# Two engines make the low words' integers, and GpSimd scales both heads' value products

## The chip, the cores and the metric

The kernel runs on one core of one Trainium2 chip. The metric is the device time of one execution in microseconds (us). The engines are named as in the profile: PE is TensorE (matmuls; PEld its weight loads), DVE is VectorE, ACT is ScalarE, POOL is GpSimd, and SP is the engine that only issues DMAs here. Each engine works through its own queue in order; between engines, semaphores hold an instruction back until what it needs is done.

## The reference

```python
# attention: 8 batches, 8 heads, 576 tokens, head size 64, all float32
scores = scale * np.matmul(q, k.transpose(0, 1, 3, 2))
thresh = np.max(scores, axis=-1, keepdims=True) - tau
scores = np.where(scores >= thresh, scores, -1000000000.0)
scores = scores - np.max(scores, axis=-1, keepdims=True)
attn = np.exp(scores)
attn = attn / (np.sum(attn, axis=-1, keepdims=True) + 1e-09)
attn_out = np.matmul(attn, v)
# heads joined: x is 4608 x 512; w_in 512 x 2048 and w_out 2048 x 512 come as float64
h = np.maximum(x @ w_in, 0.0)
return (h * h @ w_out).astype(np.float32)
```

## The kernel before

The kernel has two halves. The first is attention, the second a feed-forward layer on nine blocks of 512 tokens, whose matrix products are cut into sums and products of blocks (lines 813 to 867 for the hidden layer, 931 to 993 for the output).

Attention is a software pipeline written out by hand. A pair of heads and a block of 128 queries make a unit; two units, A and B, make one period, and `period(p)` runs for p from -2 to 74. A period issues its steps in the order of a list of names: `CONVERTING` in the periods in which a chunk of the weights is converted (p = 2 to 34), `PLAIN` in the others. This order is the order of each engine's queue; nothing reorders it later. The steps that matter here are:

- `SA`, `SB`: score products of the units A and B on PE (line 434). `topA0` to `topB1`: DVE takes each head's extreme value from PSUM and copies the scores to SBUF (line 452). `leastA`, `leastB`: POOL adds tau (line 459). `powA0` to `powB1`: the exponentials on ACT (line 462). `maskA0` to `maskB1`: DVE multiplies by the threshold's mask and sums the row (line 467).
- `over`, `inv`: POOL adds 1e-9 to the sums of the period before, and DVE takes the reciprocal (lines 474, 477).
- `U`, `V`, `W`: PE turns the weights of earlier units into PSUM (line 380), `eU`, `eV`, `eW`: ACT copies them to SBUF (line 523). `T`, `eT`: the same for queries and keys (lines 398, 403, 411); `eT` also asks for later loads.
- `PV`: the value products on PE, into PSUM banks 0 and 5 (line 532), the banks from which `topA0` and `topA1` read. `x`: they are scaled by the reciprocals, which lie in `wT` behind the turned weights (lines 640 to 646). `xm`: POOL's part of the scaling, and the stores of the result (lines 649 to 658).
- `fetch`, `c1` to `c6`: conversion of the weights from float64 to float32, one chunk of 128x512 in a period, 32 chunks in all (m = 0 to 31, begun in period m + 2). The chunk lies in SBUF as pairs of 32-bit words, low and high. `c1` takes the absolute value of the high words (ACT, line 205), `c3` clamps it (POOL, line 219), `c4` shifts it left by three (DVE, line 227), `c5` joins it with sign and top bit (DVE, line 235). `c2` makes an integer out of the top three bits of the low word, by a multiplication with 2^-29 (ACT, line 212). `c6` adds the two as integers (POOL, line 245), into the weights' place or into a tile that SP then stores.

In a converting period one of the two value products is copied by ACT and multiplied by POOL, and the other is multiplied by DVE straight from PSUM. `raw` (the two words) has four buffers, `a` (the high word) three, `x` two.

Of the kernel before, what the change touches and what calls it, by code (L numbers as in the profile page):

```python
# [11 lines left out]
I32 = mybir.dt.int32  # L12
U32 = mybir.dt.uint32
ALU = mybir.AluOpType
AF = mybir.ActivationFunctionType
# [33 lines left out]
def kernel(  # L49
# [25 lines left out]
    nc = tc.nc  # L75
    B, H, S, D = q.shape
    P = 128
# [25 lines left out]
    sb, cv = Region(arena, 0, X_AT[0]), Region(arena, X_AT[0], ARENA)  # L103
# [49 lines left out]
    WC = 512  # L153
# [16 lines left out]
    blocks_out = [(m, k) for k in RAW for m in RAW]  # L170
    chunks += [(W_OUT, m, k, out_blocks[m, k]) for m, k in blocks_out[:EARLY]]
    is_wide = moe_w_in.dtype != FP32
    raws, parts = {}, {}

    def weight(m):
        return weight_tile(*chunks[m][0:3])
# [32 lines left out]
    def convert2(m):  # L209
        if m in parts:  # L210
            lo = parts[m][0]
            nc.scalar.activation(out=lo, in_=lo.bitcast(U32), func=AF.Copy, bias=0.0, scale=2.0**-29)

    def convert3(m):
        if m not in parts:
            return
        a = parts[m][2].bitcast(FP32)
        low, high = (0x38000000, 0x47EFFFFF)
        nc.gpsimd.tensor_scalar(  # L219
            out=a, in0=a, scalar1=as_float(high), scalar2=as_float(low), op0=ALU.min, op1=ALU.max  # L220
        )

    def convert4(m):
        if m not in parts:
            return
        lo, hi, a = parts[m]
        nc.vector.tensor_scalar(
            out=a, in0=a, scalar1=3, scalar2=0x3FFFFFFF, op0=ALU.logical_shift_left, op1=ALU.bitwise_and
        )
# [255 lines left out]
    wT = {}  # L485

    TURNS = {}
    for g in range(2, 2 * len(pairs)):
        two, x = divmod(g - 4, 4)
# [4 lines left out]
    SCALE_AT = 10  # L494
# [4 lines left out]
    def fill(m, f, pt, at=None):  # L499

        first, count = FILLS[f]
        if m not in wT:
            wT[m] = sb.tile([P, (2 * CH + 2) * P], FP32, tag="wT", bufs=W_RING, name="wT")
        for i, (u, c) in enumerate(FIRST[first : first + count]):
            half_turn(pt, i, weights[2 * m + u][:, c, :, :].rearrange("p j d -> p (j d)"), at)
        if f == "W":
            rs = smalls.pop(m)
            for j in range(2):
                for r in range(2):
                    rows = ds(r * HALF, HALF)  # L510
                    for u in range(2):
                        one = rs[rows, 3, 2 * u + j : 2 * u + j + 1]
                        wide = bass.AP(tensor=one.tensor, offset=one.offset, ap=[one.ap[0], [0, D]])
                        to = pt[ds(u * D, D), r, ts(count + j, HALF)]
                        made = nc.tensor.matmul(to, wide, ident[rows, rows], start=True, stop=True)  # L515
                        touch("turns", made, at and at + r * BANK, BANK)

    def filled(m, f, pt, at=None):

        first, count = FILLS[f]  # L520
        count += 2 * (f == "W")
        to = wT[m][:, ds(weight_at(first) * P, count * P)]
        touch("weights", nc.scalar.copy(joined(to), whole(pt, 0, count)), at, 2 * BANK, m)  # L523
# [15 lines left out]
    def valued(m):  # L539

        for u in range(2):
            n = 2 * m + u
            weights.pop(n)
            if units[n][1] == FULL:
                for i in units[n][0]:
                    loaded_v.pop(i)
                    if i + 3 < len(pairs):
                        load_v(i + 3)
# [10 lines left out]
    def has(n):  # L559
        return 0 <= n < NU  # L560
# [5 lines left out]
    def sums_due(p):  # L566

        return p > max(starts) and not converts(p)
# [14 lines left out]
    def converts(p):  # L583
        return is_wide and (has_chunk(p) or has_chunk(p - 1))

    def has_chunk(p):
        return p in starts

    def begun(n):
        return starts.get(n)  # L590
# [4 lines left out]
        maskB1  # L595
    """.split()
    CONVERTING = """
        fetch U SA s1 eU over topA1 topA0 leastA SB c1 topB0 V c2 PV topB1 powA1 powA0
        eV powB1 maskA1 T leastB inv c3 powB0 W maskA0 x c4 maskB1 c5 maskB0 c6 xm eT eW
    """.split()  # L600

    def spots():
        return [(sc[:, ds(b * BANK + REST, (FULL + 1) * HALF)], b * BANK) for b in (1, 4)]

    def middle():
        return sc[:, 2 * BANK : 4 * BANK].rearrange("p (r n) -> p r n", r=2)

    def period(p):

        A, B_, a, b = 2 * p, 2 * p + 1, 2 * p - 2, 2 * p - 1  # L610
        m, turns = p - 2, TURNS.get(p, ())
        late, pt = {"W": []}, {}

        def fills(f, m):
            if has(2 * m):
                pt[f] = pt_pool.tile([P, 2, BANK], FP32, tag="pt", name="pt")
                fill(m, f, pt[f])

        def evict(f, m):
            if has(2 * m):  # L620
                filled(m, f, pt[f], 2 * BANK if f == "W" else None)

        def W():
            if has(2 * m + 2):
                pt["W"] = middle()
                fill(m + 1, "W", pt["W"], 2 * BANK)

        def turn_some():
            late["turn"] = [turn(g // 2, g % 2, spots()) for g in turns]

        def PV():
            if has(2 * m):
                values(m)

        def values_out():
            if not has(2 * m):
                return
            late["x"] = x = sb.tile([P, 2, P], FP32, tag="x", bufs=2, name="x")
            for j in range(2):
                from_ = sc[:, ds(5 * j * BANK, P)]  # L640
                if converts(p) and j == 0:
                    made = nc.scalar.copy(x[:, j, :], from_)
                else:
                    made = nc.vector.tensor_tensor(  # L644
                        out=x[:, j, :], in0=from_, in1=wT[m][:, ts(SCALE_AT + j, P)], op=ALU.mult
                    )
                touch("x", made, 5 * j * BANK, P, m)

        def given_out():
            if has(2 * m):  # L650
                x = late.pop("x")
                if converts(p):
                    mine = x[:, 0, :]
                    nc.gpsimd.tensor_tensor(out=mine, in0=mine, in1=wT[m][:, ts(SCALE_AT, P)], op=ALU.mult)
                wT.pop(m)
                valued(m)
                give_x(m, x)
            ask(False)

        def scored_a():  # L660
            if has(A):
                scores(A, False)
                scores(A, True)
                scores(B_, True)
                softmax(A)

        def scored_b():
            if has(A):
                scores(B_, False)
                softmax(B_)  # L670

        def every(key):
            for then in late.get(key, ()):
                then()

        steps = {
            "U": lambda: fills("U", m), "V": lambda: fills("V", m + 1), "W": W, "T": turn_some,
            "eU": lambda: evict("U", m), "eV": lambda: evict("V", m + 1), "eW": lambda: evict("W", m + 1),
            "eT": lambda: every("turn"),
            "SA": scored_a, "SB": scored_b,  # L680
            "PV": PV, "x": values_out, "xm": given_out,
            "c1": lambda: convert1(begun(p)), "c2": lambda: convert2(begun(p)),
            "c3": lambda: convert3(begun(p - 1)), "c4": lambda: convert4(begun(p - 1)),
            "c5": lambda: convert5(begun(p - 1)), "c6": lambda: convert6(begun(p - 1)),
            "s1": lambda: sums_due(p) and sums_step(), "s2": lambda: sums_due(p) and p < 60 and sums_step(), "fetch": lambda: fetch(begun(p + 2)),
        }
        steps["over"] = lambda: do(a, "over")
        steps["inv"] = lambda: do(a, "inverse")
        for letter, n in (("A", A), ("B", B_)):
            for what, name in (("least", "least"),):  # L690
                steps[what + letter] = lambda n=n, name=name: do(n, name)
            for what, name in (("top", "top"), ("pow", "power"), ("mask", "mask")):
                for j in range(2):
                    steps[f"{what}{letter}{j}"] = lambda n=n, name=name, j=j: do(n, name, j)
        for name in CONVERTING if converts(p) else PLAIN:
            steps[name]()
        for n in (A, B_):
            if has(n) and units[n][1] == FULL:
                for i in units[n][0]:
                    turned.pop(i)  # L700
# [489 lines left out]
def as_float(bits):  # L1190
    import struct

    return struct.unpack("<f", struct.pack("<I", bits))[0]
# [30 lines left out]
```

## Time and profile before

| what | value |
|---|---|
| median of 2 runs | 1316.74 us (1316.07 to 1317.4) |
| profiled execution, its own time | 1314.57 us |
| span of its profile | 1312.8 us, 47885 instructions |
| busy over the span: PE / DVE / ACT / POOL | 1271.9 / 1007.1 / 855.8 / 872.0 us |
| TensorE clock granted | 0.999 of full speed |
| line 212 (c2) | 32 times, first at 24.6 us, last at 252.0 us |

The profile is of one execution. A group of instructions is shown by line, engine, operation, and what it writes and reads; then the count, the busy time in us and the mean in ns of one, and the idle time of the engine ahead of them with what ended it. Almost all SBUF tiles are parts of one tensor, `arena`, and `wall` holds the weights. A row of the timeline gives start and duration in us.

### The profile page before, as it was taken

To read this page: it belongs to the slowest core of one execution; us is meant where nothing else is said; L and a number is where in the kernel's file an instruction comes from. 1 tells how busy PE (TensorE), PEld (TensorE's weight loads), DVE (VectorE), ACT (ScalarE), POOL (GpSimd) and SP (SyncE) were. 2 spreads that over 40 slices of the span, in tenths; PEclk is the share of its full clock that TensorE was granted. 3 is DMA by queue.
4 is the path that set the end of the run, shared out by engine and by line. 5 is a ranking of instruction groups with operands and counts; after the bars stand their busy time and mean duration, and the time that the engine had idled before them with its cause. 6 is when DMAs were issued, how large, how long until landed. Compare 5 with 4: busy or idle time off the path is not lost.

```text
span 1312.8 us, 47885 instructions
## 1 busy us (share of the span) xinstructions
PE 1271.9 (97%) x19483; PEld 1142.1 (87%) x19483; DVE 1007.1 (77%) x2464; ACT 855.8 (65%) x1497; POOL 872.0 (66%) x991
## 2 busy tenths in 40 slices
PE   8998989899999999999999999999999999999998
PEld 5666666677777777999999999999999999999998
DVE  5999999999999996877887788777656654665463
ACT  6999999988999986566756675665524322432240
POOL 1556555565555421778887888758777777777775
PEclk9999999999999999999999999999999999999999
DMA  5465566544433312466556655669745224522411
GB/s 150 105 176 153 153 177 179 153 113 103 99 78 84 79 42 47 148 209 198 183 184 209 200 188 176 194 229 387 260 161 161 63 99 162 161 65 97 161 33 33
DMA packets 247035, 192.12 MB, mean 146 GB/s; under 512 B 97184, under 2 KB 195488, under 8 KB 246816
## 3 DMA queue, kind: packets, MB, share of 16 engines
q1 hardware_dynamic: 245504, 188.66, 47.6%
q8 instruction: 153, 2.51, 0.8%
q14 instruction: 66, 0.54, 0.1%
q10 hardware_dynamic: 1312, 0.41, 0.1%
HBM read 116.65 MB, written 72.35 MB: 144 GB/s over the span
## 4 chain that ended last, share of the span: by engine, by line
PE 74%; DVE 7%; issue 6%; ACT 3%; POOL 3%; DMA 3%; SPq 0%; POOLq 0%; DVEq 0%; ACTq 0%
PE ph L825 30%; PE po L960 29%; PE sc L532 6%; PE sc L434 5%; DVE arena L452 4%; PE pt L380 3%; POOL arena L219 2%; DVE arena L467 2%; ACT arena L462 1%; ACT arena L523 1%; DVE arena L235 1%; PE sc L398 1%; DMA xT<-arena 1%; PE sc L515 1%; DMA wall<-w 1%
## 5 line engine op out<-in xcount | busy, mean ns | idle before, releaser
L125 POOL TENSOR_TENSOR arena<-arena 128x512 f32<-128x512 f32 (+1 forms) x314 | 378.1, 1223 | 133.6 <-DVE arena L125 115.8
L960 PE MATMUL po<-wall,arena 128*128 128x128 f32 x3528 | 394.8, 275 | 1.4 <-ACT arena L737 1.4
L960 PEld LDWEIGHTS po<-wall,arena 128*128 128x128 f32 x3528 | 394.3, 192 | 1.9 <-ACT arena L737 1.8
L825 PE MATMUL ph<-arena,wall 128*128 128x128 f32 x3528 | 394.2, 275 | 0.7 <-DVE arena L644 0.7
L825 PEld LDWEIGHTS ph<-arena,wall 128*128 128x128 f32 x3528 | 394.0, 192 | 0.8 <-issue 0.8
L125 DVE TENSOR_TENSOR arena<-ph,arena 128x512 f32<-128x512 f32 x378 | 256.4, 689 | 86.2 <-PE ph L825 65.4
L122 POOL TENSOR_TENSOR arena<-arena 128x128 f32<-128x128 f32 (+2 forms) x314 | 254.8, 812 | 49.1 <-DMA arena<-w 32.9
L125 DVE TENSOR_TENSOR arena<-po,arena 128x128 f32<-128x128 f32 x378 | 108.4, 290 | 167.8 <-PE po L960 163.4
L467 DVE SCALAR_TENSOR_TENSOR arena<-arena 128x576 f32<-128x576 f32 x288 | 229.5, 818 | 0.7 <-POOL arena L459 0.5
L462 ACT ACTIVATE arena<-arena 128x576 f32<-128x576 f32 x288 | 207.9, 772 | 15.6 <-DVE arena L452 11.4
L452 DVE TENSOR_SCALAR_CACHE_REDUCE arena<-sc 128x576 f32<-128x576 f32 x288 | 205.4, 751 | 15.8 <-ACT arena L523 4.6
L771 ACT COPY c<-arena 128x512 f32<-128x512 f32 (+1 forms) x303 | 174.0, 581 | 50.2 <-DVE arena L122 41.5
L532 PEld LDWEIGHTS sc<-arena 64*64 64x64 f32 x5760 | 153.7, 133 | 50.1 <-DVE arena L452 37.2
L532 PE MATMUL sc<-arena 64*64 64x128 f32 (+1 forms) x5760 | 169.8, 262 | 19.4 <-DVE arena L452 18.8
L122 DVE TENSOR_TENSOR arena<-arena,c 128x512 f32<-128x512 f32 (+1 forms) x267 | 175.1, 664 | 6.2 <-ACT c L771 4.1
L434 PE MATMUL sc<-arena 64*64 64x64 f32 (+1 forms) x2304 | 167.1, 414 | 6.7 <-ACT arena L403 4.0
L523 ACT COPY arena<-pt 128x1024 f32<-128x1024 f32 x144 | 146.1, 1015 | 27.0 <-PE pt L380 26.7
L737 ACT COPY arena<-po 128x128 f32<-128x128 f32 x63 | 16.7, 265 | 186.2 <-PE po L960 183.4
L459 POOL TENSOR_SCALAR arena<-arena,tau_p 128x2 f32<-128x2 f32 x144 | 74.8, 520 | 81.1 <-DVE arena L452 77.9
L380 PEld LDWEIGHTS pt<-ident,arena 64*128 64x128 f32 x2304 | 83.4, 138 | 43.9 <-ACT arena L523 27.5
L737 ACT COPY arena<-ph 128x512 f32<-128x512 f32 x63 | 36.7, 582 | 123.5 <-PE ph L825 122.9
L380 PE MATMUL pt<-ident,arena 64*128 64x64 f32 x2304 | 102.6, 228 | 5.9 <-ACT arena L523 4.7
(50 smaller groups left out, 892.0 us busy)
## 6 DMA issues: line engine op xcount, KB each, us to landing
g<-arena SPq DMA_DIRECT2D x144, 256.0 KB, 2.6
arena<-g SPq DMA_DIRECT2D x144, 256.0 KB, 4.4
w<-arena SPq DMA_DIRECT2D x60, 256.0 KB, 2.4
wall<-w SPq DMA_DIRECT2D x49, 256.0 KB, 5.2
arena<-w SPq DMA_DIRECT2D x44, 256.0 KB, 3.3
arena<-in_v_dram SPq DMA_DIRECT2D x32, 288.0 KB, 3.8
out_dram<-arena SPq DMA_DIRECT2D x70, 128.0 KB, 2.2
arena<-in_q_dram SPq DMA_DIRECT2D x64, 128.0 KB, 3.5
```

What stands on the lines that cost most here:

```text
L122: e.tensor_tensor(out=out, in0=x, in1=y, op=ALU.subtract)
L125: e.tensor_tensor(out=out, in0=x, in1=y, op=ALU.add)
L380: made = nc.tensor.transpose(pt[:, r, ts(slot, HALF)], of[rows, :], ident[rows, rows])
L434: made = nc.tensor.matmul(sc[at, ds(to, count)], lhs, kT[rows, ds(at_k, count)], start=True, stop=True)
L452: made = nc.vector.tensor_scalar(out=s[:, j, :], in0=sc[:, ds(at, S)], scalar1=1.0, scalar2=None, op0=ALU.mult, op1=ALU.min, accum_out=nmx ...
L462: nc.scalar.activation(out=w[:, :, j, :], in_=of(j), func=AF.Exp, bias=nmx[:, j : j + 1], scale=-1.0)
L467: nc.vector.scalar_tensor_tensor(out=w[:, :, j, :], in0=of(j), scalar=thr[:, j : j + 1], in1=w[:, :, j, :], op0=ALU.is_le, op1=ALU.mult, a ...
L523: touch("weights", nc.scalar.copy(joined(to), whole(pt, 0, count)), at, 2 * BANK, m)
L532: made = nc.tensor.matmul(sc[ds(u * D, D), ds(5 * j * BANK + row, count)], loaded_v[i][rows, (c - (u != j)) % CH, :], wT[m][rows, ds(weigh ...
L771: nc.scalar.copy(c, y)
L825: nc.tensor.matmul(to[:, j, :], W_IN[m, k][:, ts(j, P)], of[k][:, m - 1, :], start=(not more and j == 0), stop=True, skip_group_check=True,)
L960: nc.tensor.matmul(to, g[:, j, :], w[:, j, :], start=(not more and j == 0), stop=(j == 3), skip_group_check=True)
```

## The change

`c2` of each chunk becomes five instructions. ACT writes its integer to a tile `t` (one buffer) instead of in place. POOL makes the same integer from the same low word by a multiplication, in place over the low word. POOL subtracts ACT's integer from its own, DVE shifts the difference left by 24, and POOL adds the shifted difference to the low word's integer, which `c6` adds to the high word one period later.

In converting periods both value products are copied by ACT, and POOL multiplies both at once (128x256 instead of 128x128); DVE's multiplication is left out there. `c3` works on the chunk begun in the same period instead of the one before. The list `CONVERTING` has another order, among other things with `c2` behind `c5` and `eV` and ahead of `maskB1`, with `T` ahead of `SB`, `over` behind `leastA`, and `inv` behind `c4`. `PLAIN` and the second half are as they were; `convert_out` has no chunks left to convert, since all 16 of `w_out` are among the 32.

```diff
--- before.py
+++ after.py
@@ -170,7 +170,7 @@
     blocks_out = [(m, k) for k in RAW for m in RAW]
     chunks += [(W_OUT, m, k, out_blocks[m, k]) for m, k in blocks_out[:EARLY]]
     is_wide = moe_w_in.dtype != FP32
-    raws, parts = {}, {}
+    raws, parts, differs = {}, {}, {}
 
     def weight(m):
         return weight_tile(*chunks[m][0:3])
@@ -209,7 +209,15 @@
     def convert2(m):
         if m in parts:
             lo = parts[m][0]
-            nc.scalar.activation(out=lo, in_=lo.bitcast(U32), func=AF.Copy, bias=0.0, scale=2.0**-29)
+            t = cv.tile([P, WC], I32, tag="t", bufs=1, name="t")
+            differs[m] = t
+            nc.scalar.activation(out=t, in_=lo.bitcast(U32), func=AF.Copy, bias=0.0, scale=2.0**-29)
+            nc.gpsimd.tensor_scalar(out=lo, in0=lo.bitcast(U32), scalar1=2.0**-29, scalar2=None, op0=ALU.mult)
+            nc.gpsimd.tensor_tensor(out=t, in0=lo, in1=t, op=ALU.subtract)
+            nc.vector.tensor_scalar(
+                out=t, in0=t, scalar1=24, scalar2=-1, op0=ALU.logical_shift_left, op1=ALU.bitwise_and
+            )
+            nc.gpsimd.tensor_tensor(out=lo, in0=lo, in1=t, op=ALU.add)
 
     def convert3(m):
         if m not in parts:
@@ -595,8 +603,8 @@
         maskB1
     """.split()
     CONVERTING = """
-        fetch U SA s1 eU over topA1 topA0 leastA SB c1 topB0 V c2 PV topB1 powA1 powA0
-        eV powB1 maskA1 T leastB inv c3 powB0 W maskA0 x c4 maskB1 c5 maskB0 c6 xm eT eW
+        fetch SA U eU T SB topA0 s1 c1 topA1 topB0 c3 V PV leastA over powA0 topB1
+        powA1 powB0 c4 eT inv x maskA1 maskA0 W leastB maskB0 c5 eV c2 powB1 c6 eW maskB1 xm
     """.split()
 
     def spots():
@@ -638,7 +646,7 @@
             late["x"] = x = sb.tile([P, 2, P], FP32, tag="x", bufs=2, name="x")
             for j in range(2):
                 from_ = sc[:, ds(5 * j * BANK, P)]
-                if converts(p) and j == 0:
+                if converts(p):
                     made = nc.scalar.copy(x[:, j, :], from_)
                 else:
                     made = nc.vector.tensor_tensor(
@@ -650,8 +658,8 @@
             if has(2 * m):
                 x = late.pop("x")
                 if converts(p):
-                    mine = x[:, 0, :]
-                    nc.gpsimd.tensor_tensor(out=mine, in0=mine, in1=wT[m][:, ts(SCALE_AT, P)], op=ALU.mult)
+                    both = x[:, :, :].rearrange("p j n -> p (j n)")
+                    nc.gpsimd.tensor_tensor(out=both, in0=both, in1=wT[m][:, ds(SCALE_AT * P, 2 * P)], op=ALU.mult)
                 wT.pop(m)
                 valued(m)
                 give_x(m, x)
@@ -680,7 +688,7 @@
             "SA": scored_a, "SB": scored_b,
             "PV": PV, "x": values_out, "xm": given_out,
             "c1": lambda: convert1(begun(p)), "c2": lambda: convert2(begun(p)),
-            "c3": lambda: convert3(begun(p - 1)), "c4": lambda: convert4(begun(p - 1)),
+            "c3": lambda: convert3(begun(p)), "c4": lambda: convert4(begun(p - 1)),
             "c5": lambda: convert5(begun(p - 1)), "c6": lambda: convert6(begun(p - 1)),
             "s1": lambda: sums_due(p) and sums_step(), "s2": lambda: sums_due(p) and p < 60 and sums_step(), "fetch": lambda: fetch(begun(p + 2)),
         }
```

## The prediction

> **What bounds the kernel now.** I read the busy table of the page first, then the windows of the two halves of attention, because the change only touches periods in which weight chunks are converted.
>
> ```profile
> PE 1271.9 (97%) x19483; PEld 1142.1 (87%) x19483; DVE 1007.1 (77%) x2464; ACT 855.8 (65%) x1497; POOL 872.0 (66%) x991
> ```
> ```profile
> 45.00:265.00 220.00, 197.84 (x5171) 140.81 (x5168) 209.26 (x602) 212.33 (x367) 129.06 (x180) 1.00 0.58 161
> 270.00:500.00 230.00, 226.29 (x5977) 170.28 (x5973) 221.69 (x661) 205.33 (x319) 113.47 (x162) 1.00 0.36 83
> ```
>
> The columns of the second fence are window, length, and busy time of PE, PEld, DVE, ACT, POOL. Over the whole span PE looks like the bound; from 45 to 265 us, where chunks are converted, it is not: ACT is busy 212.3 of 220 us and DVE 209.3, PE only 197.8. POOL is busy 129.1, so 90.9 us idle.
>
> ```profile
> L212 ACT ACTIVATE arena<-arena x32: 652/722/755, 24.6 to 252.0; 128x512 int32<-128x512 uint32 x32
> ```
>
> The step that is changed (c2, line 212) runs 32 times, first at 24.6 and last at 252.0 us. One converting period is therefore (252.0 - 24.6)/31 = 7.34 us. Per period (30 of them in 220 us) ACT works 7.08 us, DVE 6.98, POOL 4.30; POOL is idle 3.03 us. So there is some 0.3 us of slack on ACT and DVE, and 3 us on POOL.
>
> ```profile
> L219 POOL TENSOR_SCALAR arena<-arena 128x512 f32<-128x512 f32 x30 | 34.3, 1145 | 0.0
> L459 POOL TENSOR_SCALAR arena<-arena,tau_p 128x2 f32<-128x2 f32 x60 | 30.0, 499 | 31.5 <-DVE arena L452 28.8
> L245 POOL TENSOR_TENSOR arena<-arena 128x512 int32<-128x512 int32 x15 | 23.1, 1540 | 28.4 <-DVE arena L235 26.5 <-DMA arena<-in_k_dram 1.9
> L654 POOL TENSOR_TENSOR arena<-arena 128x128 f32<-128x128 f32 x30 | 13.6, 452 | 0.0
> ```
>
> These groups of POOL in that window are the price list. Last I read one period in the timeline, for the spacing of the instructions on one engine and the hand-offs between engines.
>
> ```profile
> 182.32 0.25 ACT L642 COPY arena<-sc 128x128 f32<-128x128 f32 x1
> 182.65 0.43 DVE L227 TENSOR_SCALAR arena<-arena 128x512 int32<-128x512 int32 x1 [0.30 <-POOL arena L219]
> 182.95 1.02 ACT L523 COPY arena<-pt 128x1024 f32<-128x1024 f32 x1
> 183.00 0.81 DVE L467 SCALAR_TENSOR_TENSOR arena<-arena 128x576 f32<-128x576 f32 x1
> ...
> 184.34 0.81 DVE L467 SCALAR_TENSOR_TENSOR arena<-arena 128x576 f32<-128x576 f32 x1
> 184.45 0.70 ACT L212 ACTIVATE arena<-arena 128x512 int32<-128x512 uint32 x1
> 184.51 1.53 POOL L245 TENSOR_TENSOR arena<-arena 128x512 int32<-128x512 int32 x1 [1.89 <-DVE arena L235]
> ...
> 185.08 0.75 DVE L452 TENSOR_SCALAR_CACHE_REDUCE arena<-sc 128x576 f32<-128x576 f32 x1
> ...
> 185.75 0.75 DVE L452 TENSOR_SCALAR_CACHE_REDUCE arena<-sc 128x576 f32<-128x576 f32 x1
> ...
> 186.57 2.36 PE L532 MATMUL sc<-arena 64*64 64x64 f32 x108 [0.71 <-DVE arena L452]
> ...
> 186.88 0.29 POOL L459 TENSOR_SCALAR arena<-arena,tau_p 128x2 f32<-128x2 f32 x1
> ...
> 188.04 0.72 POOL L459 TENSOR_SCALAR arena<-arena,tau_p 128x2 f32<-128x2 f32 x1 [0.87 <-DVE arena L452]
> ```
>
> What to see: DVE starts 0.03 us after the POOL result it waits for (181.47 + 1.15 to 182.65); a line 227 holds DVE 0.35 us until the next start, a mask (467) 0.74, a maximum (452) 0.67; the value products (532) start 0.82 us after the start of the second maximum and take 2.36 us. No step of today's c2 waits for POOL: the integer is one ACT instruction and is next read a period later.
>
> **The change, part by part.**
>
> *Value products.* The second 128x128 scaling leaves DVE (line 644, 8.6 us over 30, so 0.29 us) and becomes an ACT copy (line 642, 0.25 us). POOL's multiplication grows from 128x128 (0.45 us) to 128x256. Its price lies between 0.45 and twice that; between 0.45 at 128 elements and 1.28 at 512 (line 122 in the timeline at 308 us) a straight line gives 0.73, which I take. ACT would come to 7.33 us per period, just its present length.
>
> *Difference step.* Per chunk three POOL instructions of 128x512 and one DVE instruction come in. DVE's shift has the form of line 227: 0.43 us, 0.35 between starts. POOL's subtraction and addition are integer two-input operations like line 245: upper end 1.54. That row starts 0.17 us after a mask starts on DVE, and behind a mask POOL is slower (line 459: 0.29 us beside a maximum, 0.72 beside a mask, 0.43 more), so the lower end is 1.54 - 0.43 = 1.11; line 122's 1.28 lies between. I take 1.4. POOL's multiplication (uint32 to int32) appears in no row; line 219, one input, takes 1.15 beside a mask and so 0.72 without; the conversion could add up to line 245's 1.54. I take 1.0, nearer to line 219.
>
> POOL's work per period: 4.30 + (0.73 - 0.45) + 1.0 + 2 x 1.4 = 8.4 us, where 7.34 were available. At the upper prices it is 9.2. That alone ends the cover of 3.03 us.
>
> The Trainium skill (GPSIMD Engine Reference, section 3.1) puts a two-input GpSimd operation at some 2.6 cycles per element; as an estimate at its 1.2 GHz that is 1.11 us for 512 elements, the lower end above, and the loop below would be 0.3 us shorter with it.
>
> *The waits are dearer than the work*, as c2 now stands before the last mask. POOL's multiplication writes in place over the low words that ACT's c2 reads, so it waits for ACT's c2. The DVE shift waits for POOL's subtraction, and behind the shift on DVE stand maskB1 and all maxima of the next period. POOL's addition waits for the shift. From the end of one subtraction to the next:
> - hand-off 0.03, shift 0.35, maskB1 0.74, topA0 0.67, and 0.82 from topA1's start to the value products: 2.61 us. The products write the banks that these two maxima read, so they can't start sooner.
> - value products 2.36: 4.97.
> - hand-off 0.05 (taken), two ACT copies x, 0.15 between starts (182.32 to the next ACT start at 182.47): 5.32.
> - eV, which stands ahead of c2 on ACT: 0.95 of its 1.02; then c2 0.72: 6.99. All other ACT work (powers, eT, eU, c1) fits into the 4.97 us before x.
> - hand-off to POOL 0.08 (line 235's end to line 245's start), multiplication 1.0, 0.1 to the dependent one, subtraction 1.4: 9.57 us.
>
> POOL's own queue in the meantime: addition, c6, the scaled products, c3, leastA, over, leastB, from 0.5 us after the subtraction: 1.4 + 1.5 + 0.73 + 1.15 + 0.29 + 0.23 + 0.72 = 6.0, so it reaches the multiplication at 6.5, before ACT releases it at 7.1. DVE gets `over` at about 5.8 and does inv, three masks and c5 (0.09 + 3 x 0.74 + 0.61) by 8.7, before the shift is due at 9.6. So the mixed loop sets the period.
>
> *Other moves.* c3 moves into the chunk's own period, off DVE's path: line 227 loses its 0.30 us wait (9.2 us over 31). That is inside the new loop's slack, hence nothing. T, eT and the loads issued in them come earlier, `over` and leastA later: DVE idles until `over` anyway. SP's queue: the stores behind c6 and xm wait longer, but x and the raw chunk have two and four buffers, and all loads are two periods ahead; without that cover it would cost a transfer's 2 to 4 us once.
>
> **The sum.** 9.57 - 7.34 = 2.23 us per period, times 32 chunks = 71 us. 1314.6 us (the profiled execution, span 1312.8) + 71 = 1386; the median of the two runs lies 2.2 us above the profiled one, so 1388. With lower prices (0.72 and 1.11) the loop is 9.0 us: +53, 1370. With upper ones (1.54 and 1.54) 10.25: +93, 1410. The periods after line 252 us and the second half (PE at 100%) are untouched.
>
> **The rivals.**
> 1. *POOL and DVE shut each other out.* Line 459's 0.29 against 0.72 is such a case. With POOL nearly always at work, four masks, c4 and c5 would each hold a POOL instruction up: POOL's chain at full rows is 1.15 + 0.29 + 0.23 + 0.72 + 1.15 + 1.54 + 0.5 + 1.54 + 1.54 + 0.73 = 9.4 us with three such delays in it; three more of 0.43 make 10.7. +3.35 x 32 = 107: 1424 us. Against it: in the loop above the masks fall where POOL does small work or waits. The Trainium skill (SBUF — State Buffer, "Who interferes with whom") states this as a rule: a DVE instruction with two SBUF inputs and a GpSimd one that reads SBUF block each other for a whole instruction. Line 459 agrees; whether a long POOL instruction holds a mask back as fully isn't in these rows.
> 2. *POOL's added work is short.* If multiplication and subtraction took 0.45 and 0.7 us (a 128x128's price plus a little), the loop is 7.07 + 1.25 = 8.3 us: +31, 1348. For it: a part of line 245's 1.54 is waiting. Against it: line 122 takes 1.28 with no mask beside it.
> 3. *Not slower.* The integers are wanted only a period later (c6), so the chain might hide in POOL's 3.03 idle us, with DVE and ACT still setting 7.34. Place: the shift's wait on DVE. This decides if c2's end to the shift's start costs under 7.34 - 7.07 = 0.27 us. For it: POOL at 59%. Against it: the order in DVE's queue puts the next maxima behind that wait. It would give about 1317, or 1308 if also the 0.3 us waits for line 219 go.
> That the difference is all zeros would not change the time: every instruction still runs.
>
> **How the numbers follow.** Forecast 0.72 (its own range 1362 to 1412), rival 1 0.17, rival 2 0.07, rival 3 0.04. The predicted time is the forecast's, 1388 us. The range 1350 to 1425 takes in rival 1 and most of rival 2. A measurement tells about 2% here, 1290 to 1343 us: faster 0.02, same 0.05, slower 0.93.
>
> **What would show it.** Right: the new shift starts 9.3 to 10.2 us after its predecessor; DVE's largest wait in 45 to 300 us is this shift on POOL's subtraction; POOL's multiplication waits for ACT's c2; ACT and DVE fall to some 75% busy there; the windows of the last 900 us keep their shape. The step on the loop is wrong if POOL shows no idle time ahead of the multiplication (POOL's own chain then bounds), and the sizes are wrong if the subtraction isn't 1.1 to 1.55 us. A period under 8 us would refute the forecast.

## The result, and the profile after

The changed kernel takes 1433.93 us (median of 2 runs, 1432.61 to 1435.26) against 1316.74 us: ratio 1.0889, 95% interval 1.0863 to 1.0915. The profiled execution has a span of 1430.7 us, 117.9 more than before. It is slower, as forecast, but 46 us beyond the predicted 1388 and 9 us outside the range.

First two lines of the page: busy time of PE over the whole span, and the clock that TensorE was granted in 40 equal slices.

```profile
PE 1331.0 (93%) x19483; PEld 1192.4 (83%) x19483; DVE 1019.5 (71%) x2463; ACT 862.7 (60%) x1530; POOL 1011.9 (71%) x1087
...
PEclk9988899878899999999999999999999999999999
```

Before, every digit of the clock was 9. Now PE is 59 us longer busy with the same 19483 matmuls, and sevens and eights of the clock stand among the first eleven slices, which hold the converting periods.

The windows of attention after the change (window, length, busy time of PE, PEld, DVE, ACT, POOL, then the granted clock):

```profile
45.00:265.00 220.00, 165.49 (x3503) 121.48 (x3506) 152.82 (x412) 150.17 (x269) 178.19 (x185) 0.90 0.40 102
...
420.00:620.00 200.00, 197.37 (x5236) 148.80 (x5227) 192.29 (x580) 178.51 (x277) 94.78 (x137) 1.00 0.34 79
```

In the converting stretch ACT and DVE fell from 212.3 and 209.3 of 220 us to 150.2 and 152.8: neither is the bound any more. POOL is busy 178.2 us, yet idle for 42. Once no chunk is left (420 to 620 us) PE is busy 99% of the time at clock 1.00, as it was before in such periods (226.3 of 230 us).

The new shift (line 217) with what its engine waited for, from the view of one line (minimum, median, maximum in ns; first and last start):

```profile
L217 DVE TENSOR_SCALAR arena<-arena x32: 426/427/429, 34.7 to 375.0; 128x512 int32<-128x512 int32 x32
its engine sat idle before it (us, times) until:
  POOL arena L216: 83.4, 32
```

The shift waits 2.6 us per chunk for POOL's subtraction. POOL's multiplication (line 215) takes 1.60 to 2.08 us, 1.65 in the median, and waits 1.5 us per chunk for ACT's c2. A period is (375.0 - 34.7)/31 = 10.98 us on average, where 9.57 was forecast. In stretches at full clock it is 9.95. One such period in the timeline:

```profile
193.60 0.43 ACT L650 COPY arena<-sc 128x128 f32<-128x128 f32 x2
193.92 1.03 ACT L531 COPY arena<-pt 128x1024 f32<-128x1024 f32 x1
194.82 0.71 ACT L214 ACTIVATE arena<-arena 128x512 int32<-128x512 uint32 x1
195.61 1.60 POOL L215 TENSOR_SCALAR arena<-arena 128x512 int32<-128x512 uint32 x1 [0.55 <-ACT arena L214]
...
195.66 1.23 DVE L475 SCALAR_TENSOR_TENSOR arena<-arena 128x576 f32<-128x576 f32 x1
...
197.30 1.36 POOL L216 TENSOR_TENSOR arena<-arena 128x512 int32<-128x512 int32 x1
...
198.69 0.43 DVE L217 TENSOR_SCALAR arena<-arena 128x512 int32<-128x512 int32 x1 [1.17 <-POOL arena L216]
199.03 0.81 DVE L475 SCALAR_TENSOR_TENSOR arena<-arena 128x576 f32<-128x576 f32 x1
199.20 1.81 POOL L220 TENSOR_TENSOR arena<-arena 128x512 int32<-128x512 int32 x1 [0.54 <-DVE arena L217]
...
199.91 0.20 PEld L388 LDWEIGHTS pt<-ident,arena 64*128 64x128 f32 x4 [1.97 <-DVE arena L475]
```

This is the loop of the prediction, in its order: copies x (650), eV (531), c2 (214), multiplication, subtraction, shift, maskB1. The last line is new to the argument: PE, which has to turn the weights that maskB1 makes, waits 2 us for it.

The other periods differ from this one almost only in the value products (line 540). The same 70 of them in a period at half clock and in this one, and the windows around the two, where the third column from the end is the granted clock:

```profile
90.38 3.77 PE L540 MATMUL sc<-arena 64*64 64x128 f32 x70 [0.25 <-DVE arena L460]
191.32 2.19 PE L540 MATMUL sc<-arena 64*64 64x128 f32 x70 [0.25 <-DVE arena L460]
```
```profile
90.30:93.70 3.40, 3.32 (x64) 3.32 (x67) 2.33 (x9) 2.24 (x5) 3.24 (x6) 0.50 0.10 19
191.00:194.00 3.00, 2.53 (x75) 2.15 (x74) 2.04 (x7) 2.88 (x8) 2.94 (x6) 1.00 0.08 17
```

From topA1's start to the end of the value products it is 3.01 us in the periods at full clock, 3.94 on average over 31 periods, and up to 4.9. These 0.93 us are most of the 1.03 between 9.95 and 10.98. That the 2 us waits bring the low clock is what e1_warm tests.

### The profile page after: what moved, and what is told of

It is laid out like the page before. It is cut to its first block, busy times and chain, and to the rows that moved or that the text cites. A ratio compares the mean times of both kernels' runs of the same rounds, so it can differ in the third digit from the quotient of the medians.

```text
span 1430.7 us, 47995 instructions
## 1 busy us (share of the span) xinstructions
PE 1331.0 (93%) x19483; PEld 1192.4 (83%) x19483; DVE 1019.5 (71%) x2463; ACT 862.7 (60%) x1530; POOL 1011.9 (71%) x1087
## 4 chain that ended last, share of the span: by engine, by line
PE 72%; ACT 7%; POOL 7%; issue 5%; DVE 4%; DMA 3%; SPq 0%; DVEq 0%; ACTq 0%
PE ph L833 27%; PE po L968 25%; PE sc L540 10%; PE sc L442 5%; POOL arena L215 4%; PE pt L388 4%; POOL arena L216 3%; ACT arena L531 2%; DVE arena L460 2%; DVE arena L475 2%; ACT arena L470 2%; ACT arena L214 2%; DMA wall<-w 1%; PE sc L406 1%; PE sc L523 1%
## 5 line engine op out<-in xcount | busy, mean ns | idle before, releaser
L540 PEld LDWEIGHTS sc<-arena 64*64 64x64 f32 x5760 | 189.4, 154 | 43.1 <-DVE arena L460 26.7
L540 PE MATMUL sc<-arena 64*64 64x128 f32 (+1 forms) x5760 | 213.1, 293 | 5.9 <-DVE arena L460 5.0
L442 PE MATMUL sc<-arena 64*64 64x64 f32 (+1 forms) x2304 | 175.4, 414 | 13.6 <-ACT arena L531 9.3
L388 PEld LDWEIGHTS pt<-ident,arena 64*128 64x128 f32 x2304 | 89.7, 145 | 106.8 <-DVE arena L475 67.7
L388 PE MATMUL pt<-ident,arena 64*128 64x64 f32 x2304 | 113.5, 237 | 65.6 <-DVE arena L475 63.4
L442 PEld LDWEIGHTS sc<-arena 64*64 64x64 f32 x2304 | 69.6, 135 | 57.2 <-issue 19.2
L467 POOL TENSOR_SCALAR arena<-arena,tau_p 128x2 f32<-128x2 f32 x144 | 80.8, 561 | 44.8 <-DVE arena L460 41.0
```

What stands on the lines that cost most here:

```text
L388: made = nc.tensor.transpose(pt[:, r, ts(slot, HALF)], of[rows, :], ident[rows, rows])
L442: made = nc.tensor.matmul(sc[at, ds(to, count)], lhs, kT[rows, ds(at_k, count)], start=True, stop=True)
L540: made = nc.tensor.matmul(sc[ds(u * D, D), ds(5 * j * BANK + row, count)], loaded_v[i][rows, (c - (u != j)) % CH, :], wT[m][rows, ds(weigh ...
```

## The experiments

Theory A is the loop (with PE inside it); rival B is that POOL's work and its collisions with DVE set the period. Nine kernels were run. Times are medians; each ratio is to runs of the kernel before on the same chip. Those runs have medians of 1315.5 to 1317.5 us, so differences in us between experiments are good to 2 or 3 us.

**e1_warm: keep PE at work.** In `fills`:

```diff
+                if f == "V" and converts(p):
+                    for _ in range(16):
+                        nc.tensor.transpose(pt[f][:, 0, 0:P], ident[:, :], ident[:, :])
                 fill(m, f, pt[f])
```

> Sixteen transposes of the identity go into V's PSUM tile just ahead of V's own, in converting periods, where PE waits 2 us for maskB1; nothing else changes. Theory A (the loop from the subtraction over the next maxima, the value products and c2 back to the subtraction sets the period, and its PE part is slowed by the half clock that PE's idle time brings): the granted clock stays at 1.0 in the converting stretch, the period is 9.95 us everywhere instead of 10.98 on average, and the time is 1434 - 32 x 1.03 = 1401 us, ratio to the kernel before 1.064. Rival B (GpSimd's chain and its collisions with VectorE set the period, the low clock is a by-product): the clock rises, the time stays at 1425 to 1440 us.

Measured: 1407.23 us, ratio 1.0686 (1.0669 to 1.0703). The same window of the changed kernel (first fence) and of e1_warm:

```profile
60.00:260.00 200.00, 152.67 (x3180) 111.68 (x3174) 136.75 (x368) 137.79 (x248) 160.61 (x168) 0.89 0.42 107
```
```profile
60.00:260.00 200.00, 180.98 (x3742) 131.78 (x3734) 151.84 (x393) 147.09 (x263) 172.67 (x179) 1.00 0.44 113
```

The clock goes from 0.89 to 1.00 and the time falls by some 27 us, although PE has 16 operations more in every period. Most periods are 9.96 us, every fourth or fifth 10.6, the mean is 10.1. So the low clock was not a by-product: PE's part of the loop ran slower, and this cost 27 of the 117 us. The other 90 are the longer loop itself: (10.1 - 7.34) x 32 = 88 us.

**e2_no_chain: everything but the difference.** `c2` is again the single ACT instruction of before, at its new place.

> Only the difference step is taken back: c2 is again the one ScalarE instruction in place, at its new place in the list. The new order of the list, c3 in the chunk's own period and the value products scaled by GpSimd stay. This leaves out the difference's addition into the weights. Theory A: without the wait on the shift the period is set by ScalarE's work, 7.3 us, the clock stays at 1.0, time 1310 to 1322 us, ratio 0.995 to 1.004. Rival C (the new order of the list costs by itself): periods of 8 us or more, 1340 us or more.

Measured: 1326.50 us, ratio 1.0074 (1.0057 to 1.0090). The difference step and the waits it brings carry almost the whole loss. But the rest is not free: the period (from c6 to c6) is 7.68 us throughout, where before it was 7.26 in most cases and 7.33 on average. The timeline shows where:

```profile
161.75 1.04 POOL L245 TENSOR_TENSOR arena<-arena 128x512 int32<-128x512 int32 x1 [2.81 <-DVE arena L235]
162.15 1.25 DVE L467 SCALAR_TENSOR_TENSOR arena<-arena 128x576 f32<-128x576 f32 x1 [0.49 <-ACT arena L462]
```

maskB1 waits 0.49 us for powB1, which now stands behind c2 on ACT; in the meantime POOL's c6 starts, and the mask takes 1.25 us instead of 0.81. It ends at 163.40, 0.61 us after c6 (162.79).

**e6_pow_first: as e2_no_chain, with powB1 ahead of c2.**

```diff
-        ... maskB0 c5 eV c2 powB1 c6 eW maskB1 xm
+        ... maskB0 c5 eV powB1 c2 c6 eW maskB1 xm
```

> As e2_no_chain (no difference step), with the last exponential powB1 ahead of c2 on ScalarE instead of behind it. Theory D: the 0.39 us per period that e2_no_chain loses are GpSimd's c6, which starts before maskB1 because maskB1 waits for powB1; with powB1 early maskB1 follows c5 at once, the period is 7.25 to 7.4 us and the time 1312 to 1319 us. Rival: ScalarE's larger work (7.35 us and the hand-offs around it) sets 7.65 us, and the time stays at 1324 to 1329 us.

Measured: 1314.13 us, ratio 0.9986 (0.9976 to 0.9996), period 7.28 us on average. The masks of e2_no_chain (first) and of e6_pow_first, from 60 to 260 us (busy, mean ns, idle before):

```profile
L467 DVE SCALAR_TENSOR_TENSOR arena<-arena 128x576 f32<-128x576 f32 x105 | 94.1, 930 | 10.7 <-ACT arena L462 10.7
```
```profile
L467 DVE SCALAR_TENSOR_TENSOR arena<-arena 128x576 f32<-128x576 f32 x109 | 92.3, 880 | 5.1 <-ACT arena L462 4.9
```

Per period (a quarter of the count) the wait for powB1 falls from 0.41 to 0.19 us and four masks from 3.72 to 3.52: together 0.42 us, about the whole difference. I had expected the collision with c6 to be gone. It is gone in about every second period, and full in the others, so that periods of 6.8 and 7.7 us mostly alternate. Two maskB1 in successive periods:

```profile
161.97 1.48 DVE L467 SCALAR_TENSOR_TENSOR arena<-arena 128x576 f32<-128x576 f32 x1 [0.26 <-ACT arena L462]
169.32 0.80 DVE L467 SCALAR_TENSOR_TENSOR arena<-arena 128x576 f32<-128x576 f32 x1
```

The first still waits for powB1 and meets c6 (161.80 to 162.84); the second follows c5 at once. Of the new order of the list, this one step costs the 9 us; the larger ACT work isn't to blame.

**e3_split: all instructions, without the wait.** Shift and addition move to a step of their own, `c2b`, called with `begun(p - 1)`, that is for the chunk one period older (the two instructions follow there unchanged):

```diff
+    def convert2b(m):
+        if m in parts:
+            lo, t = parts[m][0], differs[m]
...
-        ... V PV leastA over powA0 topB1
+        ... V PV leastA over powA0 topB1 c2b
```

> All instructions of the change stay, but shift and addition are done for the chunk one period older, the shift behind topB1 on VectorE, where the subtraction has long ended; the multiplication and the subtraction stay where they are. Theory A: VectorE no longer waits, GpSimd's own work is left as the bound: 1.63 + 1.3 + 1.3 to 1.8 + 1.03 + 0.73 + 0.79 + 0.23 + 2 x 0.3 to 0.9 = 7.6 to 9.3 us, clock at 1.0, time 1325 to 1380 us. Rival B (GpSimd's work and its collisions with VectorE set the period): still 9.9 us or more, 1400 us or more.

Measured: 1393.51 us, ratio 1.0580 (1.0564 to 1.0596): better by 40 us, but neither theory's number. DVE no longer waits for the subtraction; instead its masks have become long:

```profile
L479 DVE SCALAR_TENSOR_TENSOR arena<-arena 128x576 f32<-128x576 f32 x98 | 120.3, 1261 | 5.3 <-ACT arena L474 5.3
```
```profile
193.56 1.29 POOL L224 TENSOR_TENSOR arena<-arena 128x512 int32<-128x512 int32 x1
193.61 1.86 DVE L479 SCALAR_TENSOR_TENSOR arena<-arena 128x576 f32<-128x576 f32 x1
```

The mask starts 0.05 us after POOL's addition and ends at 195.47, 0.62 us after the addition's end at 194.85, where a mask alone takes 0.81: most of its work came after POOL was done. The wait that was taken away came back as collisions. The clock isn't back to full either: 0.91 from 60 to 260 us, against 0.89 in the changed kernel.

**e5_split_one_input: the same, with masks that read one tensor.** The threshold is left out in the converting periods.

> As e3_split, but in converting periods VectorE's four masks read one SBUF tensor (the weights times one, summed) instead of two; this leaves the threshold out there. Theory D (what is left in e3_split is masks and GpSimd's instructions shutting each other out: 1.26 us a mask against 0.81): masks at 0.75 to 0.82 us, VectorE busy 7 us per period, the period 7.6 to 8.1 us with GpSimd's own work (1.62 + 1.3 + 1.3 + 1.03 + 0.73 + 0.61 + 0.23 + 0.6 = 7.4 us) as the bound, clock at 1.0, time 1325 to 1345 us. Rival: the masks are long for another reason, or GpSimd's work and waits set e3_split's 9.7 us: over 1375 us.

Measured: 1361.00 us, ratio 1.0346 (1.0329 to 1.0363), clock 1.0, period 8.83 us. The masks are 0.74 us now, where e3_split had 1.26, and 33 us are won, so the collisions were real (theory D); but the forecast was 1325 to 1345. The clock also rose from 0.91 to 1.00, and what each of the two gave wasn't separated. What remained:

```profile
L215 POOL TENSOR_SCALAR arena<-arena 128x512 int32<-128x512 uint32 x23 | 47.8, 2076 | 12.2 <-ACT arena L214 12.2
```

The multiplication takes 2.08 us, since c5, which still reads two tensors, runs beside its start, and c2 waits 1.5 us for POOL's addition, as `t` has one buffer. POOL is busy 182.7 of 200 us and waits 12.2 us for c2, which has itself been waiting for POOL: here POOL's queue with this wait is the bound.

**e4_f32_mult: the multiplication without conversions.**

> GpSimd's multiplication takes the clamped float32 high words (dense) times zero and writes float32 over the low words, in place of the conversion from uint32 to int32; ScalarE's factor is zero too, so the three lowest bits of the weights are left out. All instructions, their places and waits stay. Theory A with the price of the multiplication as the mis-sized term (1.63 us where 1.0 was taken): it takes 0.8 to 0.9 us without the conversions, the undisturbed period falls from 9.95 to 9.1 to 9.2 us, the time by at least 26 us to 1395 to 1408 us. Rival: the two conversions cost nothing and the 1.63 us is waiting for VectorE: period and time as they were.

Measured: 1427.86 us (1421.70 to 1433.62), ratio 1.0857 (1.0815 to 1.0898): hardly a gain, and the expectation missed.

```profile
169.26 0.69 DVE L245 SCALAR_TENSOR_TENSOR arena<-arena 128x512 int32<-128x512 int32 x1
169.87 1.62 POOL L215 TENSOR_SCALAR arena<-arena 128x512 f32<-128x512 f32 x1 [1.93 <-issue]
171.57 1.29 POOL L218 TENSOR_TENSOR arena<-arena 128x512 int32<-128x512 int32 x1
172.90 0.43 DVE L219 TENSOR_SCALAR arena<-arena 128x512 int32<-128x512 int32 x1 [2.95 <-POOL arena L218]
```

Float32 to float32 takes 1.62 us too (1.54 to 1.62 where nothing disturbs it), with DVE at rest from 169.95 on. So the price is neither the conversion nor a collision.

**e7_dense_mult: a multiplication in a dense tile.**

> GpSimd's multiplication works in place on the dense float32 high words (times one) instead of on every second word of the low words; ScalarE makes the integer in place, the subtraction takes the low words from themselves. The weights come out as in the kernel before. All other instructions stay, but the wait for c2 moves from the multiplication to the subtraction. Theory E (the multiplication is dear since it writes every second word): it takes 0.6 to 0.8 us, the period falls to 8.3 to 8.7 us, time 1350 to 1385 us. Rival F (a multiplication by a scalar is dear in any layout): 1.5 to 1.65 us, period 9.2 to 9.5 us without the low clock, time 1380 to 1415 us.

Measured: 1385.91 us, ratio 1.0534 (1.0519 to 1.0549), period 9.60 us. The multiplication takes 1.94 us, not theory E's 0.6 to 0.8. It now runs beside two masks, which may hold it up, so this run alone doesn't show what the layout costs; e9_warm_min does. The time is in rival F's range, the period 0.1 above it. The multiplication no longer waits for c2, and the clock from 60 to 260 us is 0.96 instead of 0.89; which share of the gain each has wasn't tried.

**e9_warm_min: another operation in its place.**

> As e1_warm (full clock), but GpSimd's multiplication is replaced by minimum and maximum with zero of the dense float32 high words, written over the low words; ScalarE's factor is zero, so the three lowest bits of the weights are left out. Theory F (the operation is what is dear: a multiplication by one scalar 1.6 us, a minimum with a maximum 0.6 us): 0.6 to 0.8 us, the period falls from 9.97 to 9.0 to 9.3 us, the time from 1407 to 1375 to 1387 us. Rival: writing every second word, or the place behind c2, costs the 1.6 us, and period and time stay within 0.2 us and 6 us of e1_warm.

Measured: 1398.12 us, ratio 1.0621 (1.0604 to 1.0639). POOL's stand-in for the multiplication (first fence) and DVE's c5, 60 to 260 us:

```profile
L215 POOL TENSOR_SCALAR arena<-arena 128x512 f32<-128x512 f32 x21 | 17.6, 840 | 14.1 <-POOL arena L469 14.1
```
```profile
L245 DVE SCALAR_TENSOR_TENSOR arena<-arena 128x512 int32<-128x512 int32 x20 | 31.1, 1553 | 0.0
```

Theory F holds for the price: 0.69 us in the median (0.84 on average) instead of 1.65, at the same place. e4_f32_mult reads and writes the same tiles in the same layout with a multiplication and takes 1.54 to 1.62, so neither the layout nor the place is what is dear. But only 9 us came of it, not 20 to 32. With a shorter first instruction, POOL's subtraction starts before c5 does; c5 then takes 1.55 us on average instead of 0.82 in e1_warm, and the shift stands behind it on DVE. The mean period (from shift to shift) is 9.84 us instead of 10.12: POOL's part of the loop got 0.9 us shorter, and the collisions took its place at nearly the same length.

**e8_before_c3: the kernel before, with c3 directly behind over.**

```diff
-        fetch U SA s1 eU over topA1 ... leastB inv c3 powB0 ...
+        fetch U SA s1 eU over c3 topA1 ... leastB inv powB0 ...
```

> The kernel before with one step moved: c3 (still of the chunk one period older) directly behind over, so that c4 no longer waits for it on VectorE. If those 0.30 us per period are on the path: period 7.0 to 7.15 us, 1308 to 1313 us, ratio 0.993 to 0.998. Rival: ScalarE's 7.08 us of work takes over at once, and the ratio is 0.998 to 1.001.

Measured: 1310.67 us, ratio 0.9964 (0.9951 to 0.9978): the fastest of all versions, by 0.36%, with an interval that stays below 1. c4 no longer waits, from 60 to 260 us:

```profile
L227 DVE TENSOR_SCALAR arena<-arena 128x512 int32<-128x512 int32 x27 | 11.2, 414 | 0.0
```

Undisturbed periods are 6.87 to 7.06 us instead of 7.26, but some are over 8, so that the mean falls only from 7.33 to 7.25. Why those are long was not tried.

## Why the prediction was wrong, point by point

- **The loop** was right in kind. From the subtraction's end to the multiplication's start it gave 7.07 us; measured, from 188.71 (187.38 + 1.33, the subtraction a period earlier) to 195.61, it is 6.90. DVE's waits, POOL's wait for c2 and the untouched second half came as said; the shift comes 9.3 to 10.2 us after its predecessor only in the periods at full clock.
- **The multiplication, taken at 1.0 us**, was mis-sized: 1.60 to 1.65 in most periods, above the upper bound of 1.54. I took line 219 as the nearest row since it is a one-input operation of the same shape; e4 and e9 show that the operation decides, a minimum with a maximum 0.61 to 0.79 us, a multiplication by a scalar 1.6. The subtraction, taken at 1.4, was 1.29 to 1.36, so the sign that I had named for wrong sizes watched the wrong instruction. The loop is thus 9.95 instead of 9.57 us: (9.95 - 7.34) x 32 = 84 us where the sum had 71.
- **The value products, taken at 2.36 us as before**, are the step that failed. That row was measured on a PE that was busy 197.8 of 220 us at clock 1.00. The change makes PE wait 2 us in every period, the clock falls, and the products run at half clock in part of the periods. From topA1's start to their end the sum had 0.82 + 2.36 = 3.18 us; measured, it is 3.01 at full clock, close to the sum, and 3.94 on average. The mean period becomes 10.98 us: (10.98 - 7.34) x 32 = 116 us, close to the measured difference of 117.9 in the spans. e1_warm shows the cause by its converse: with PE kept at work the clock is 1.00 and the time 1407 us. The prediction took the row as if the clock could not change, and had no rival for it either.
- **Neither error alone leaves the range.** Without the low clock e1_warm stands at 1407 us; with it, but with the multiplication at 1.0 us, the sum would be 1388 + 33 = 1421 (an estimate: 1.03 us x 32 added to the forecast). Together they pass the upper end of 1425.
- **Rival 1** (masks and POOL shut each other out) gave 1424 us, and that this is near the result is chance: e1_warm ends at 1407 with all collisions left. They are a second bound just below the loop, as e9_warm_min shows (9.84 us), and so shortening the loop's POOL part alone helps little. That masks "fall where POOL does small work or waits" was wrong: maskB0 runs beside the multiplication and takes 1.23 us (195.66), and POOL's addition beside maskB1 takes 1.81 (199.20) where 1.4 was taken. Neither lies on the loop.
- **The new order at no cost** was wrong by 9 us when the difference is left out (e2), because powB1 stands behind c2. In the changed kernel maskB1 stands behind the shift and takes 0.81 us (199.03), so there these 9 us are covered.
- c3's earlier place was costed at nothing because the loop hides it. The trace agrees: behind c4 DVE still idles 1.07 us until POOL's `over` (the wait of `inv` at 194.11). e8 shows what such a move is worth where nothing hides it: 0.36%.

## What to carry to other kernels

When a change lengthens a loop through several engines, ask what the others do while they wait: here a TensorE that idled for some 2 us in every 10 to 12 lost clock, and the durations of the old profile no longer held for it. Price an instruction by a row with the same operation, not just the same shape and number of inputs. And before taking a wait away, look for the next bound: here the loop at full clock (10.1 us) and the bound by collisions (9.84) lay within 0.3 us of each other, and e3_split and e9_warm_min, which each removed a real cost, gave back part of the gain.

## What the hardware showed unexpectedly

- The clock dropped without any long pause. The longest single wait of PE's queue for a mask from 60 to 360 us was 2.4 us, and PE was still about 75% busy (165.5 of 220 us). Windows of 10 us between 100 and 170 us show granted clocks of 0.66 to 0.91, and the window from 90.3 to 93.7 one of 0.50. The Trainium skill (TensorE: Matmul & The Clock Gate, "Why this matters for your kernels") advises no idle gaps over some 3 us between bursts. Here waits of some 2 us, one in each period, were enough, and the measurement decides; 16 transposes of the identity in the gap kept the clock at 1.00. Gap length isn't all of it: from 172 to 210 us waits of 1.8 to 2.1 us left the clock at 0.99. What sets these periods apart stays open.
- A DVE mask that arrives while a two-input POOL instruction runs ends 0.61 to 0.62 us after that instruction, whether it started 0.40 us after it (e2_no_chain, 162.15) or 0.05 (e3_split, 193.61). The Trainium skill (SBUF — State Buffer, "Who interferes with whom") says that a DVE instruction with two SBUF inputs and a GpSimd one that reads SBUF block each other; these rows agree, and e5_split_one_input, where the masks read one, agrees as well. Beside POOL's multiplication the block was not whole, and there the measurement differs from the page: the mask that began 0.05 us after it ended 0.32 us before it (195.66 + 1.23 against 195.61 + 1.60).
- One scalar multiplication of 128x512 on GpSimd takes 1.62 us with VectorE at rest (e4_f32_mult), a minimum and a maximum in one instruction 0.61 (c3 in e2_no_chain). Why they differ stays open.
